# Tying a unit's attention scores behind the output of the unit two ahead

## The chip, the cores and the metric

One core of a Trainium2 chip runs the whole program. The metric is the device time of one execution in microseconds. The engines are TensorE (PE, with its weight loads as PEld), VectorE (DVE), ScalarE (ACT), GpSimd (POOL) and SyncE (SP), each with a queue of its own that it works off in order.

## The reference, cut to what matters

```python
# 1. attention: batch 4, 8 heads, 576 positions, head size 64
scores = q @ k.T / sqrt(64)
# heads 0-3: only the last 32 positions count ("local")
# heads 4-7: only positions of the same residue mod 32, not later ("strided")
attn = softmax(where(mask, scores, -1e9))
x = attn @ v                      # 2304 tokens x 512
# 2. a gated network: rms norm, 512 -> 2 x 1536 -> 512
xn = x / sqrt(mean(x*x) + 1e-6) * rms_g
x = (silu(xn @ w_gate) * (xn @ w_val)) @ w_out
# 3. a mixture of 8 experts, the best one for each token, 512 -> 1024 -> 512
out = p_e * (relu(x @ w1[e]) @ w2[e])
```

## The kernel before, in words

Attention is cut into 48 units, 12 for each batch: first six of the strided heads, then six of the local ones. A unit is a pair of heads and a group of 2, 3 or 4 tiles. In every tile the masked-out blocks are left out: a strided tile has 54 keys (L179 writes 64 x 54 scores), a local one 96 (64 x 96). The four steps of a unit are functions of their own:

- `scores`: two matmuls for each tile (one per head), from the tile `qk` into a PSUM bank (L179, `s<-qk` or `pt<-qk` in the profile); DVE adds the mask and takes the maximum (L189), ACT takes the exponential (L199). It also issues a later unit's load on SP's queue.
- `norm`: DVE divides by the sum (L220 to L222).
- `transpose`: a PE transpose for each tile (L228), and an ACT copy into the tile `ptS` (L230).
- `output`: two matmuls for each tile, `ptS` against `v` (L238, `mx<-ptS,v` or `o<-ptS,v`); ACT copies the result into the tile that the network reads (L247, L253).

The matmuls of attention are plain fp32, and each leaves two records in the trace: the 8 matmuls of a unit with 4 tiles are 16 records. The contraction of an output is over the keys, 54 or 96 rows; that of the scores over 64 rows.

The network works on nine chunks j of 256 tokens, each with 12 blocks f: `gate_val` is 24 matmuls of 256 columns (L472 to L474), `gelu_post` runs on ACT and DVE, `ff_out` is 6 matmuls of 512 columns (L497 to L499), two blocks later. These are called the main stream below. Units 0 to 11 are worked before it starts; units 12 to 47 are woven into it: three times in each block a `slot` is traced, which takes one or no piece from the list of `att_sequence`. Units 12 to 23 are the first such list (scores in the one bank `pt`, transposes and outputs in `mx`), 24 to 47 the second (scores in `s0` and `s1` in turn, transposes in `pt`, outputs in `mx`). In the list, two units ahead:

```python
for n in range(len(fs) + AHEAD):
    m = n - AHEAD + 1
    def piece(n=n, m=m):
        if 0 <= m < len(fs):
            fs[m][1]()           # norm of unit n-1
        if n < len(fs):
            fs[n][0]()           # scores of unit n
    seq.append(piece)
    if n >= AHEAD:
        seq += fs[n - AHEAD][2:] # transpose and output of unit n-2
```

An output can carry a number `after`: it isn't taken from the list before that chunk's inputs have been traced, since it overwrites a tile that they read. The order in which each engine gets its instructions isn't the order of tracing. A scheduler sets it before the run: by its own estimate of times it takes, for each engine, the instruction traced first among those that are ready. `tc.high_priority()` puts what is traced in it ahead of everything; `tc.issue_after(ins)` queues what is traced in it, on the engine of `ins`, behind `ins`, without waiting for its end. PE then works its queue strictly in that order, and an instruction that must wait for another engine holds all behind it.

Of the kernel before, what the change touches and what calls it, by code (L numbers as in the profile page):

```python
# [33 lines left out]
LQ, LK, SQ = 64, 64 + WIN, 3 * LEN  # L34
# [14 lines left out]
def moe_kernel(  # L49
# [17 lines left out]
    V, A, G, T, SP = nc.vector, nc.scalar, nc.gpsimd, nc.tensor, nc.sync  # L67
# [39 lines left out]
    units = []  # L107
# [9 lines left out]
    def fill(dst, n):  # L117

        for _ in range(n):
            T.matmul(dst, ones16, ones16, start=True, stop=True)  # L120
# [3 lines left out]
    def geometry(u):  # L124

        b, p, g = units[u]
        tiles = L_TILES if p < 2 else S_TILES
        return tiles[g], sum(tiles[:g]), *((LQ, LK) if p < 2 else (SQ, SQ))

    def load_part(c):  # L130
        u = n_load[c]
        if u >= len(units):
            return
        n_load[c] += 1
        b, p, g = units[u]
        n, t0, _, nk = geometry(u)
        if c == 0:
            cols = L_COLS if p < 2 else S_COLS
            w, o = cols[g], sum(cols[:g])
            if 3 <= u < 6:  # L140
                t = xn_p.tile([128, 2 * CH], F32, tag=("xh0", "xl0", "xh1")[u - 3], name="qk_early")
            else:
                t = qkv_p.tile([128, L_COLS[0]], F32, tag="qk", name="qk", bufs=3)
            SP.dma_start(out=t[:, :w], in_=(qk_l if p < 2 else qk_s)[b, p % 2, :, o:o + w])
        else:
            if 2 <= u < 8:
                if u % 2 == 0:
                    v_pair[0] = wts.tile([128, 2, 4, 128], F32, tag=f"w{NP - u // 2}", name="v_early")
                t = v_pair[0][:, u % 2]
            else:  # L150
                t = qkv_p.tile([128, 4, 128], F32, tag="v", name="v", bufs=2)
            SP.dma_start(
                out=t[:nk, :n],
                in_=(v_l if p < 2 else v_s)[b, p % 2].rearrange("k (t d) -> k t d", d=128)[:, t0:t0 + n],
            )
        qkv_t[u, c] = t

    def attention(u, banks):

        b, p, g = units[u]  # L160
        local = p < 2
        n, t0, nq, nk = geometry(u)
        k0 = n * nq if local else n * nq + LQ - SQ
        st = {}

        def scores():
            t = qkv_t.pop((u, 0))
            pr = pp.tile([128, 4, LK], F32, tag="pr", name="pr", bufs=3)
            mx = sm.tile([128, 4], F32, tag="mx", name="mx")
            sd = sm.tile([128, 4], F32, tag="sd", name="sd")  # L170
            sps = banks("s")
            if n_fill[0] < 12:
                n_fill[0] += 1
                fill(sps[:, 384:], 10)
            sps = sps[:, :4 * LK].rearrange("p (t k) -> p t k", k=LK)
            for i in range(n):
                for h in range(2):
                    hp = slice(64 * h, 64 * h + 64)
                    T.matmul(  # L179
                        sps[hp, i, :nk],  # L180
                        t[hp, i * nq:i * nq + LQ],
                        t[hp, k0 + i * nq:k0 + i * nq + nk],
                        start=True,
                        stop=True,
                    )
            for i in range(n):
                mask = m_str if not local else (m_loc0 if g == 0 and i == 0 else m_loc)
                pv = pr[:, i, :nk]
                V.tensor_tensor_reduce(  # L189
                    out=pv,  # L190
                    in0=sps[:, i, :nk],
                    in1=mask[:, :nk],
                    op0=ALU.add,
                    op1=ALU.min,
                    scale=-0.125,
                    scalar=3.0e38,
                    accum_out=mx[:, i:i + 1],
                )
                act = A.activation(  # L199
                    out=pv,  # L200
                    in_=pv,
                    func=AF.Exp,
                    bias=mx[:, i:i + 1],
                    scale=-1.0,
                    accum_out=None if u < 12 else sd[:, i:i + 1],
                )
                if not flow_on:
                    mark[0] = act
            st["p"] = pr, sd
            if not 3 <= u < 6:  # L210
                load_part(0)
            if u < 4:
                load_part(1)

        def norm():
            pr, sd = st["p"]
            pv, sl = pr[:, :n, :nk], sd[:, :n]
            if u < 12:
                V.tensor_reduce(out=sl, in_=pv, op=ALU.add, axis=AX.X)
            V.tensor_scalar(out=sl, in0=sl, scalar1=1e-9, scalar2=None, op0=ALU.add)  # L220
            V.reciprocal(out=sl, in_=sl)
            V.tensor_tensor(out=pv, in0=pv, in1=sl.unsqueeze(2).to_broadcast([128, n, nk]), op=ALU.mult)  # L222

        def transpose():
            pr, _ = st.pop("p")
            pt = banks("t").rearrange("p (t k) -> p t k", k=128)
            for i in range(n):
                T.transpose(pt[:nk, i], pr[:, i, :nk], ident)  # L228
            ptS = st["t"] = pp.tile([128, 4, 128], F32, tag="ptS", name="ptS", bufs=2)
            A.copy(ptS[:nk, :n], pt[:nk, :n])  # L230

        def output():
            t = qkv_t.pop((u, 1))
            ptS = st.pop("t")
            ot = banks("o")
            for i in range(n):
                for h in range(2):
                    T.matmul(  # L238
                        ot[64 * h:64 * h + 64, i * nq:(i + 1) * nq],
                        t[:nk, i, 64 * h:64 * h + 64],  # L240
                        ptS[:nk, i, 64 * h:64 * h + nq],
                        start=True,
                        stop=True,
                    )
            if local:
                x = x_t[b, p, g] = xt_p.tile([128, n * LQ], F32, tag=f"x{g}", name=f"x{g}", bufs=2)
                A.copy(x, ot[:, :n * LQ])  # L247
            else:
                if g == 0:
                    x_t[b, p] = xt_p.tile([128, S], F32, tag="xs", name="xs", bufs=4)  # L250
                x = x_t[b, p].rearrange("p (j c) -> p c j", c=CLS)
                c0, c1 = 3 * t0, min(3 * (t0 + n), CLS)
                A.copy(x[:, c0:c1], ot[:, :(c1 - c0) * LEN].rearrange("p (c j) -> p c j", j=LEN))  # L253
            if not 2 <= u < 8:
                load_part(1)
            n_out[0] = u + 1


        if local and b > 0:
            output.after = (S * (b - 1) + LQ * (t0 + n) - 1) // CH  # L260
        elif not local and b > 1:
            output.after = (S * (b - 1) - 1) // CH
        return scores, norm, transpose, output

    def att_sequence(us, banks):

        AHEAD = 2
        seq = []
        fs = [attention(u, banks) for u in us]
        for n in range(len(fs) + AHEAD):  # L270
            m = n - AHEAD + 1

            def piece(n=n, m=m):
                if 0 <= m < len(fs):
                    fs[m][1]()
                if n < len(fs):
                    fs[n][0]()

            seq.append(piece)
            if n >= AHEAD:  # L280
                seq += fs[n - AHEAD][2:]
        return seq
# [403 lines left out]
    stage = [0]  # L686
    turn = {"s": 0, "t": 0, "o": 0}

    def att_banks(kind):
# [7 lines left out]
        return bank((("mx", "o1")[n % 2], "mx", "mx")[stage[0]])  # L697

    aux = att_sequence(list(range(12)), att_banks)
    aux.reverse()  # L700
    fill(bank("mx")[:, :128], 40)
# [18 lines left out]

    hold.append(r_last[0])
    stage[0] = 1
    aux = att_sequence(list(range(12, 24)), att_banks)
    aux.reverse()
    rest = att_sequence(list(range(24, len(units))), att_banks)

    def pop_aux():
        if not aux and rest:
# [533 lines left out]
```

## Time and profile before

| what | value |
|---|---|
| three runs | 874.0, 875.13 and 1648.38 us; median 875.13 us |
| the profiled execution | 872.97 us, its span from first to last instruction 871.1 us |
| PE matmuls | 850.5 us busy, 98% of the span, 6872 records |
| PE weight loads | 764.1 us busy, 88% (beside the matmuls) |
| DVE, ACT, POOL | 509.1, 382.9 and 87.4 us busy: 58%, 44%, 10% |
| granted TensorE clock | 0.99 of full speed over the span |

Busy time of an engine is the time in which one of its instructions runs. A matmul's record is longer than the distance between two of them, since they overlap: what a matmul costs is read from start to start. The highest of the three runs isn't used.

### The profile page before, as it was taken

The numbers are of one execution on the slowest core, as the hardware profiler recorded it, in microseconds if no ns is written. First come the engines' busy times: TensorE is split into PE (matmuls) and PEld (weight loads), VectorE is DVE, ScalarE is ACT, GpSimd is POOL, SyncE is SP. The second block draws the span as 40 slices with busy tenths as digits, with TensorE's granted clock in tenths as the row PEclk, the third lists the DMA queues.
The fourth block names the chain that finished last, engine by engine and source line by source line (L and its number), as shares of the span: only waits on it lengthen the run. The fifth ranks groups of instructions, "written<-read, shape, count | busy, mean of one in ns | idle before, by whom it ended". The sixth has DMA issues, their size and how long they took to land.

```text
span 871.1 us, 18007 instructions
## 1 busy us (share of the span) xinstructions
PE 850.5 (98%) x6872; PEld 764.1 (88%) x6872; DVE 509.1 (58%) x1614; ACT 382.9 (44%) x935; POOL 87.4 (10%) x87
## 2 busy tenths in 40 slices
PE   8799999999999999999999999999999999999996
PEld 7588988988888988989999999998899999999995
DVE  4989974454653553644534535347786666666651
ACT  4766553344453254442332222325455545455540
POOL 0314500000000000000000000001031111111100
PEclk9889999999999999999999999999999999999998
DMA  8969111022121011100000000033196733765000
GB/s 251 351 224 329 68 32 41 11 59 60 36 61 53 1 47 44 61 14 26 1 10 26 1 21 5 2 125 118 62 365 216 217 129 113 230 214 183 25 25 21
DMA packets 33014, 84.45 MB, mean 97 GB/s; under 512 B 5122, under 2 KB 12850, under 8 KB 32920
## 3 DMA queue, kind: packets, MB, share of 16 engines
q1 hardware_dynamic: 23064, 54.50, 19.6%
q10 hardware_dynamic: 6336, 19.26, 6.0%
q0 software_dynamic: 3520, 9.45, 3.2%
q8 instruction: 58, 0.95, 0.4%
q14 instruction: 36, 0.29, 0.1%
HBM read 91.57 MB, written 10.49 MB: 117 GB/s over the span
## 4 chain that ended last, share of the span: by engine, by line
PE 81%; issue 10%; DMA 3%; DVE 2%; POOL 1%; ACT 1%; SPq 0%; ACTq 0%; POOLq 0%
PE gv L472 12%; PE gv L473 11%; PE gv L474 11%; PE o L499 5%; PE o L497 5%; PE o L498 5%; PE o L1023 3%; PE o L1025 3%; PE o L1024 3%; PE mx L238 2%; PE s L179 2%; PE s L999 2%; PE s L1000 2%; PE s L1001 2%; PE gv L999 2%
## 5 line engine op out<-in xcount | busy, mean ns | idle before, releaser
L472 PE MATMUL gv<-xh,wf 128*128 128x256 f32 x864 | 251.7, 292 | 0.8 <-DVE t L482 0.8
L473 PE MATMUL gv<-xl,wf 128*128 128x256 f32 x864 | 245.1, 284 | 0.0
L474 PE MATMUL gv<-xh,wf 128*128 128x256 f32 x864 | 244.5, 283 | 0.0
L472 PEld LDWEIGHTS gv<-xh,wf 128*128 128x128 f32 x864 | 163.3, 189 | 9.1 <-DVE t L482 1.7
L473 PEld LDWEIGHTS gv<-xl,wf 128*128 128x128 f32 x864 | 163.4, 189 | 3.3 <-issue 0.2
L474 PEld LDWEIGHTS gv<-xh,wf 128*128 128x128 f32 x864 | 163.6, 189 | 0.6 <-issue 0.2
L966 DVE TENSOR_TENSOR l<-stg,h 128x1024 fp32r<-128x1024 f32 x88 | 107.2, 1224 | 38.8 <-ACT h L965 38.6
L481 DVE SCALAR_TENSOR_TENSOR t<-t,gv 128x256 f32<-128x256 f32 x108 | 45.2, 418 | 121.5 <-ACT t L480 120.9
L965 ACT CAST h<-stg 128x1024 fp32r<-128x1024 f32 x88 | 91.6, 1048 | 35.8 <-PE o L1025 25.9
L480 ACT ACTIVATE t<-gv 128x256 f32<-128x256 f32 x108 | 41.3, 382 | 145.8 <-PE gv L474 135.8
L497 PE MATMUL o<-wf,hh 128*128 128x512 f32 x192 | 76.9, 400 | 0.0
L485 ACT CAST hh<-t 128x256 fp32r<-128x256 f32 x108 | 43.7, 405 | 73.8 <-PE o L499 31.9
L498 PE MATMUL o<-wf,hh 128*128 128x512 f32 x192 | 75.7, 394 | 0.0
L499 PE MATMUL o<-wf,hl 128*128 128x512 f32 x192 | 75.4, 398 | 0.0
L486 DVE TENSOR_TENSOR hl<-t,hh 128x256 fp32r<-128x256 f32 x108 | 48.6, 450 | 39.3 <-ACT hh L485 37.5
L1023 PE MATMUL o<-h,hT 128*128 128x512 f32 x176 | 70.6, 401 | 0.0
L1025 PE MATMUL o<-h,hT 128*128 128x512 f32 x176 | 68.8, 391 | 0.0
L1024 PE MATMUL o<-l,hT 128*128 128x512 f32 x176 | 68.5, 389 | 0.0
L199 ACT ACTIVATE pr<-pr,mx 128x54 f32<-128x54 f32 (+1 forms) x160 | 52.5, 348 | 14.3 <-DVE mx L189 13.7
L949 POOL DMA_INDIRECT xg<-rows_d,gi x22 | 24.2, 1102 | 302.4 <-DVE gi L947 142.4
L999 PE MATMUL s<-xh,h 128*128 128x256 f32 x176 | 49.7, 282 | 0.0
L1000 PE MATMUL s<-xl,h 128*128 128x256 f32 x176 | 49.5, 281 | 0.0
(212 smaller groups left out, 1556.9 us busy)
## 6 DMA issues: line engine op xcount, KB each, us to landing
stg<-in SPq DMA_DIRECT2D x96, 512.0 KB
raw<-in ACTq DMA_DIRECT2D x36, 511.8 KB
rows_d<-x SPq DMA_DIRECT2D x18, 256.5 KB
qk<-in SPq DMA_DIRECT2D x14, 221.0 KB
qk<-in SPq DMA_DIRECT2D x8, 272.0 KB
qk<-in SPq DMA_DIRECT2D x8, 208.0 KB
v<-in SPq DMA_DIRECT2D x14, 108.0 KB
qk<-in SPq DMA_DIRECT2D x7, 167.0 KB
```

Source lines behind the costliest of these rows:

```text
L472: T.matmul(dst, wh[:, ks], xh[k], start=(k == order[0]), stop=False)
L473: T.matmul(dst, wh[:, ks], xl[k], start=False, stop=False)
L474: T.matmul(dst, wl[:, ks], xh[k], start=False, stop=(k == order[3]))
L497: T.matmul(o, h[:, ms], wh, start=(f == 0), stop=False)
L498: T.matmul(o, h[:, ms], wl, start=False, stop=False)
L499: T.matmul(o, l[:, ms], wh, start=False, stop=(f == NF - 1))
L965: A.copy(h, lt["stg", i])
L966: V.tensor_tensor(out=l, in0=lt["stg", i], in1=h.bitcast(F32), op=ALU.subtract)
L999: T.matmul(dst, w[0][:, k, cs_], xh, start=(k == 0), stop=False)
L1023: T.matmul(ys[t][m], hh, w[0][:, c], start=(q == 0 and c == 0), stop=False)
L1024: T.matmul(ys[t][m], hh, w[1][:, c], start=False, stop=False)
L1025: T.matmul(ys[t][m], hl, w[0][:, c], start=False, stop=(q == 3 and c == 1))
```

## The change: what it does

For units 12 to 47 the list has another order. The scores of unit n and the output of unit n-2 are one piece: first the output's matmuls, then the scores'. Both are traced at the highest priority, and the scores' matmuls are queued on PE behind the last matmul of the output. The transpose of unit n-2 stands in the list ahead of that piece, the normalisation of unit n-1 behind it. The first two units of a list have no output ahead in it; unit 12's scores, and those of unit 24, are queued behind the last output of the list before. `after` holds back the whole piece.

```diff
+    pv_last = [None]
+
+    def close_to(last):
+
+        near = ExitStack()
+        if stage[0]:
+            near.enter_context(tc.high_priority())
+            if last[0] is not None:
+                near.enter_context(tc.issue_after(last[0].ins))
+        return near
...
-            for i in range(n):
-                for h in range(2):
-                    hp = slice(64 * h, 64 * h + 64)
-                    T.matmul(
...
+            with close_to(pv_last):
+                for i in range(n):
+                    for h in range(2):
+                        hp = slice(64 * h, 64 * h + 64)
+                        T.matmul(
...
+            pv_last[0] = None
...
-            for i in range(n):
-                for h in range(2):
-                    T.matmul(
...
+            with close_to([None]):
+                for i in range(n):
+                    for h in range(2):
+                        pv_last[0] = T.matmul(
...
-    def att_sequence(us, banks):
+    def att_sequence(us, banks, close=False):
...
+        if close:
+
+            for n in range(len(fs) + AHEAD):
+                m = n - AHEAD
+                if m >= 0:
+                    seq.append(fs[m][2])
+
+                def both_tiles(n=n, m=m):
+                    if m >= 0:
+                        fs[m][3]()
+                    if n < len(fs):
+                        fs[n][0]()
+
+                if m >= 0 and hasattr(fs[m][3], "after"):
+                    both_tiles.after = fs[m][3].after
+                seq.append(both_tiles)
+                if 0 <= m + 1 < len(fs):
+                    seq.append(fs[m + 1][1])
+            return seq
...
-    aux = att_sequence(list(range(12, 24)), att_banks)
+    aux = att_sequence(list(range(12, 24)), att_banks, True)
...
-    rest = att_sequence(list(range(24, len(units))), att_banks)
+    rest = att_sequence(list(range(24, len(units))), att_banks, True)
```

## Rows read from the trace of the kernel before

**Rows 1.** Windows view; stretch, length, busy time (instructions) of PE, PEld, DVE, ACT, POOL:

```profile
48.00:180.00 132.00, 130.66 (x1098) 117.23 (x1097) 96.50 (x279) 67.04 (x194) 26.86 (x26) 0.99 0.32 112
180.00:455.00 275.00, 275.00 (x2418) 243.94 (x2417) 137.02 (x626) 114.57 (x380) 1.85 (x2) 1.00 0.13 37
```

**Rows 2.** Waits of PE from 48 to 455 us; total, times, longest:

```profile
PE mx L238 <- ACT ptS L230: 1.0, 1, 1.0
PE mx L228 <- ACT xs L253: 0.3, 1, 0.3
```

**Rows 3.** PE's timeline, local outputs alone; start, length, line, operands, records:

```profile
258.45 0.28 PE L474 MATMUL gv<-xh,wf 128*128 128x256 f32 x1
258.67 0.69 PE L238 MATMUL mx<-ptS,v 96*64 96x64 f32 x16
...
259.51 0.28 PE L473 MATMUL gv<-xl,wf 128*128 128x256 f32 x1
...
451.00 0.28 PE L474 MATMUL gv<-xh,wf 128*128 128x256 f32 x1
451.21 0.45 PE L238 MATMUL mx<-ptS,v 96*64 96x64 f32 x8
...
451.82 0.28 PE L473 MATMUL gv<-xl,wf 128*128 128x256 f32 x1
```

**Rows 4.** PE's timeline, scores and a strided output side by side, their alternation left out:

```profile
318.57 0.40 PE L499 MATMUL o<-wf,hl 128*128 128x512 f32 x1
318.90 0.49 PE L179 MATMUL s<-qk 64*64 64x54 f32 x9
319.18 0.26 PE L238 MATMUL mx<-ptS,v 54*64 54x54 f32 x1
...
320.19 0.28 PE L473 MATMUL gv<-xl,wf 128*128 128x256 f32 x1
```

**Rows 5.** PE's timeline, scores and a local output side by side:

```profile
375.40 0.39 PE L499 MATMUL o<-wf,hl 128*128 128x512 f32 x1
375.72 0.38 PE L179 MATMUL s<-qk 64*64 64x96 f32 x2
376.02 0.69 PE L238 MATMUL mx<-ptS,v 96*64 96x64 f32 x16
376.64 0.71 PE L179 MATMUL s<-qk 64*64 64x96 f32 x10
...
377.50 0.28 PE L473 MATMUL gv<-xl,wf 128*128 128x256 f32 x1
```

**Rows 6.** PE's timeline, the first attention piece inside the main stream:

```profile
55.64 0.44 PE L179 MATMUL pt<-qk 64*64 64x54 f32 x8
```

**Rows 7.** Timeline, transposes and the ACT copy behind them: units 17 and 31:

```profile
112.12 0.49 PE L228 MATMUL mx<-cs,pr 128*54 128x128 f32 x3
...
115.97 0.46 ACT L230 COPY ptS<-mx 54x384 f32<-54x384 f32 x1
...
254.98 0.60 PE L228 MATMUL pt<-cs,pr 128*96 128x128 f32 x4
...
255.75 0.58 ACT L230 COPY ptS<-pt 96x512 f32<-96x512 f32 x1
```

**Rows 8.** PE's timeline ahead of the main stream's first matmul:

```profile
42.36 1.10 PE L179 MATMUL pt<-qk 64*64 64x54 f32 x16 [0.51 <-ACT ptS L230]
43.39 0.69 PE L362 MATMUL gv<-cs,nr 128*128 128x128 f32 x2
44.23 1.10 PE L179 MATMUL pt<-qk 64*64 64x54 f32 x16 [0.15 <-PE gv L362]
...
45.74 0.64 PE L238 MATMUL o<-ptS,v 96*64 96x64 f32 x8
47.19 0.89 PE L179 MATMUL pt<-qk 64*64 64x54 f32 x12 [0.80 <-PE o L238]
48.01 0.80 PE L472 MATMUL gv<-xh,wf 128*128 128x256 f32 x2
```

More of the change, by code (lines that the diff above doesn't have):

```diff
@@ L175, in scores @@
             sps = sps[:, :4 * LK].rearrange("p (t k) -> p t k", k=LK)
-            for i in range(n):
-                for h in range(2):
-                    hp = slice(64 * h, 64 * h + 64)
-                    T.matmul(
[L180 to L185, printed above, removed]
+            with close_to(pv_last):
[3 more added lines that the diff above has]
+                        T.matmul(
+                            sps[hp, i, :nk],
+                            t[hp, i * nq:i * nq + LQ],
+                            t[hp, k0 + i * nq:k0 + i * nq + nk],
+                            start=True,
+                            stop=True,
+                        )
+            pv_last[0] = None
             for i in range(n):
@@ L235, in output @@
             ot = banks("o")
-            for i in range(n):
-                for h in range(2):
-                    T.matmul(
[L239 to L244, printed above, removed]
+            with close_to([None]):
+                for i in range(n):
+                    for h in range(2):
+                        pv_last[0] = T.matmul(
+                            ot[64 * h:64 * h + 64, i * nq:(i + 1) * nq],
+                            t[:nk, i, 64 * h:64 * h + 64],
+                            ptS[:nk, i, 64 * h:64 * h + nq],
+                            start=True,
+                            stop=True,
+                        )
             if local:
```

## The prediction

> **What bounds the kernel now.** I read the windows view first. TensorE (PE) is busy 130.66 of 132 us in the stretch from 48 to 180 us and 275.00 of 275 us from 180 to 455 us, while DVE and ACT have room [rows 1]. These two stretches hold every attention piece of units 12 to 47 but the scores of units 12, 13 and 14, so the second view to read is who PE waited for in them: 1.3 us in all, 1.0 of it once, for the copy of a transposed tile [rows 2]. Nothing but PE's own queue sets the time there. A main matmul less or more on PE moves the end by its own length, and so does whatever an attention piece costs PE beyond its own columns. The third view is therefore PE's timeline: how much later does the main stream come back after a piece?
>
> Main matmuls of 256 columns start 0.118 us apart, those of 512 columns 0.233 us. Take the 16 records of one output of K=96 (each fp32 matmul leaves two records): from the last main start, 258.45, to the second main start behind, 259.51, pass 1.06 us; two ordinary steps would take 0.24, so the piece cost 0.82. The same form with 8 records costs 451.82 - 451.00 - 0.24 = 0.58 [rows 3]. The difference is 0.03 us per record, which leaves 0.34 us that do not depend on the number of records: 0.17 us for going from main work into the piece and 0.17 us for coming back. Call each a change.
>
> Two places show what happens when scores and outputs stand side by side already. Strided: 16 scores and 16 outputs of K=54, mixed with one another, cost 320.19 - 318.57 - 0.35 = 1.27 us [rows 4]; 32 x 0.03 is 0.96, so two changes of 0.155 and none inside, however often the lines alternate. Local: 2 scores, 16 outputs of K=96, 10 scores cost 377.50 - 375.40 - 0.35 = 1.75 us [rows 5]; with 0.045 for a record of 96 columns (0.03 x 96/64) the columns are 12 x 0.045 + 16 x 0.03 = 1.02, and 0.73 is left, which is four changes of 0.18. So going between scores (64 rows by 64) and a local output (96 rows by 64) is a change as dear as one to main work; between scores and a strided output (54 rows by 64) it is free.
>
> The Trainium skill, "TensorEngine Tiling (Array Packing)", section "Key Properties", says that changing the tiling mode, not merely the tile, drains TensorE. Read that way it speaks against the change for the local pairs, whose two halves differ in mode; the rows agree, at 0.18 us. Were the two halves one mode, the 14 local pairs below would each save 0.17 more, 2.4 us in all.
>
> **The change part by part.** It removes and adds no matmul; it moves them. *Ties.* Scores of unit n (n from 14 to 23 and from 26 to 47) are queued on PE behind the last output matmul of unit n-2, and both are picked ahead of all main work once ready. Today each stands where the scheduler found room, and pieces are cut in two: of unit 15's 16 score records 8 stand at 55.64 [rows 6] and 8 behind later main work.
>
> Counting on PE's timeline, the attention pieces from 55.64 [rows 6] to 451.21 [rows 3] make 66 stretches between main matmuls (a stretch beside transposes counts once; the transposes themselves show no change price and stay). Eight of these have two changes inside, like [rows 5]. That is 66 x 2 + 8 x 2 = 148 changes. After: 32 pairs; 4 outputs alone (units 22, 23, 46, 47); the scores of 24 and 25 alone, since they start the second sequence; and the scores of unit 13, see below. That is 39 stretches, 78 changes, and 14 more inside the local pairs (outputs 18 to 21, 30 to 35, 42 to 45): 92. Fewer by 56, at 0.17 us: 9.5 us saved.
>
> *Scores that lose their cover.* Units 12, 13 and 14 now run at 42.36, 44.23 and 47.19, before the main stream's first matmul at 48.01 [rows 8], where PE has idle time. Unit 12's will wait behind unit 11's output (45.74) and still fit before the main stream. Unit 13's need the same PSUM bank as unit 12's, read out by DVE in between, and land inside the stream: 16 x 0.03 = 0.48 us of columns (its two changes are counted above). Unit 14's ride behind unit 12's output: 12 x 0.03 = 0.36 us. Together 0.84 us lost. Net 9.5 - 0.8 = 8.7 us.
>
> *The start itself.* Unit 12's scores at 42.36 stand ahead of the matmul that spreads the first norm (43.39), on which all of the main stream's inputs hang [rows 8]. With them gone that matmul could start up to 1.0 us earlier. Against that, unit 12's scores may now push the first main matmul back by their own length, 1.1 us. I take nothing, with both ends, -1.0 and +1.1, in the range.
>
> *The new wait.* An output at the highest priority is queued on PE directly behind the moment at which the scheduler expects the ACT copy of the transposed tile. If the copy is later on the chip, all of PE waits: main matmuls are behind it in an in-order queue. Today there is room: unit 31's transposes end at 255.58, its copy at 256.33 [rows 7], and its output starts at 258.67 [rows 3], 2.3 us behind. Such an undisturbed copy is over 0.75 us after the transposes, in some six main matmuls. A disturbed one, unit 17's, only starts 3.36 us after them (112.61 and 115.97), behind other ACT work [rows 7]. So a wait is bounded by 0 and by about 3.2 us (3.36 + 0.46 less the 0.6 that six matmuls and a start take) for each pair. The trace has one output close behind its copy, unit 12's, and it waited 1.0 us [rows 2]; all else that PE consumes in these 407 us was in time within 0.3 us [rows 2]. I lean to the many: 0.05 us for each of 32 pairs, 1.6 us.
>
> *Queues passed.* The loads that a score or output issues on SP's queue stay in program order with the piece that holds them; a score now comes two slots later and its next load with it, and three buffers cover that. The normalisation of a unit is now one slot ahead of its transposes, not four; its three small DVE instructions have a slot of 1.4 us there (a third of 24 x 0.118 + 6 x 0.233). ACT gets the output's copy and DVE the scores' maxima at once; both had idle time there [rows 1]. I cost these at nothing; if DVE's cover fails between 48 and 130 us, the first to be late is a transpose, and PE waits for it as it does for the copy.
>
> *Sum.* The profiled execution took 872.97 us (span 871.1). 872.97 - 8.7 + 1.6 = 865.9. The two runs that agree, 874.0 and 875.13, are 1.0 and 2.2 above the profiled one, so I add 1.3 and say 867 for a median.
>
> **The rivals.** *A: the wait takes the place of the gap, and the kernel is slower.* Place: the ten pairs of the first sequence (outputs 12 to 21), where DVE and ACT are busiest and copies come late. If the schedule foresees nothing of ACT's queue, each waits like unit 12's, 1.0 us: +10 against -8.7, 1.3 slower, 876. It decides from 0.87 us for each of the ten pairs, or 0.27 us for each of all 32. For it: unit 12's wait and unit 17's late copy. Against: one such wait in 407 us. Half of it, 0.15 us for every pair, gives 865.9 + 3.2 + 1.3, about 870.5.
>
> *B: the tie doesn't bind.* The edge only orders scores behind outputs; if they are not ready then (bank not yet read out by DVE, load not landed), main matmuls get in between and the pair is two stretches. Then only cut pieces are healed: 7 extra stretches and the 16 inner changes, 14 + 16 = 30 changes, 5.1 us, less 0.8 and some waits: about 871. For it: the first sequence has one scores bank. Against: a unit takes six slots there, over 8 us, and the bank's last reader is DVE at the start of that time.
>
> *C: more than forecast.* The start gains its 1.0 us, and the 1.3 us of waits [rows 2] go because less DVE work stands ahead of them; no pair waits: 872.97 - 8.7 - 2.3 + 1.3, about 863.
>
> **How the numbers follow.** Forecast 0.55 (its own range 864 to 870); A in half 0.15 (870.5); A in full, slower than before, 0.08 (876); B 0.09 (871); C 0.13 (863). The range from 862 to 875 leaves out A in full and a little on either end. Two per cent, about what a measurement of this kernel can tell from no change, is 17.5 us: no case reaches that. I keep 0.04 for faster by more (the changes would have to cost twice what the rows show), 0.03 for slower by more (waits of over 0.8 us for every pair), 0.93 within.
>
> **What would show it.** On PE's timeline scores directly behind outputs in 32 places; 16 + 16 strided records at about 1.3 us, local ones at 1.4 to 1.7 us with three changes; about 39 stretches. PE's waits for ACT's copy between 48 and 455 us at 1 to 4 us in all; 10 or more is rival A. Main matmuls between an output and its scores are rival B. The first main matmul near 48. Behind 455 us everything as before, some 7 us earlier. I am wrong if the pairs are in place and the end has not moved: then PE was not the only bound.

## The result and the profile after

The changed kernel takes 867.11 us, median of four runs (865.1 to 868.9). The kernel before has three usable runs, 874.0, 875.13 and 877.93 us, with a mean of 875.7 (a fourth was disturbed and isn't used). The ratio is 0.9902, 95% interval 0.9875 to 0.9928: 8.6 us less, between 6.3 and 10.9. Run once more later it gave 0.988 (0.9851 to 0.9909), 10.5 us less. The prediction said 867.

The head of the profile page (busy us, share of the span, instructions) shows TensorE as full as before, in a span that is 5.7 us shorter:

```profile
span 865.4 us, 18024 instructions
PE 843.9 (98%) x6872; PEld 763.8 (88%) x6872; DVE 508.9 (59%) x1614; ACT 381.5 (44%) x935; POOL 85.7 (10%) x87
```

PE has the same 6872 records and 6.6 us less to be busy with; no work was taken out, so the work itself got cheaper on PE. The windows view of the same two stretches (columns as in [rows 1]) shows where: in the same 407 us PE now gets through 3599 matmul records instead of 3516.

```profile
48.00:180.00 132.00, 129.50 (x1118) 117.68 (x1115) 97.66 (x299) 69.57 (x209) 25.09 (x26) 0.98 0.34 116
180.00:455.00 275.00, 274.69 (x2481) 247.94 (x2479) 139.55 (x631) 114.36 (x384) 1.85 (x2) 1.00 0.13 37
```

PE's timeline shows how. A strided pair, to be held against [rows 4], and then a local one, against [rows 5]:

```profile
344.27 0.28 PE L507 MATMUL gv<-xh,wf 128*128 128x256 f32 x1
344.48 0.61 PE L252 MATMUL mx<-ptS,v 54*64 54x54 f32 x13
344.88 0.26 PE L191 MATMUL s<-qk 64*64 64x54 f32 x1
...
344.98 0.52 PE L191 MATMUL s<-qk 64*64 64x54 f32 x11
345.43 0.39 PE L505 MATMUL gv<-xh,wf 128*128 128x256 f32 x1
345.65 0.28 PE L506 MATMUL gv<-xl,wf 128*128 128x256 f32 x1
...
127.83 0.28 PE L507 MATMUL gv<-xh,wf 128*128 128x256 f32 x1
128.04 0.69 PE L252 MATMUL mx<-ptS,v 96*64 96x64 f32 x16
128.66 0.71 PE L191 MATMUL pt<-qk 64*64 64x96 f32 x12
129.30 0.39 PE L505 MATMUL gv<-xh,wf 128*128 128x256 f32 x1
129.53 0.28 PE L506 MATMUL gv<-xl,wf 128*128 128x256 f32 x1
```

By the prediction's method (last main start to second main start behind, less two steps of 0.12) the strided pair costs 1.14 us: 28 records at 0.03 are 0.84, and 0.30 is left for two changes. The local pair costs 1.46: 1.02 of columns and 0.44, three changes of 0.15. Counted in PE's order from the first main matmul on, there are 38 stretches of attention with 15 inner changes, 91 changes in all, against the 148 of before; the prediction expected 39, 14 and 92. The three differences: the scores of units 24 and 25 stand together (one stretch less), output 13 and its scores are parted by main work (one more), and two pairs, with the outputs of units 34 and 35, stand in one stretch (one less, and one inner change more).

PE's waits from 48 to 455 us (total, times, longest) answer to [rows 2]:

```profile
PE gv L505 <- DVE t L515: 1.4, 2, 1.2
PE gv L505 <- ACT xh L410: 0.9, 2, 0.7
PE mx L252 <- ACT ptS L243: 0.2, 1, 0.2
```

2.5 us in place of 1.3. 0.7 of them stand in front of the very first main matmul; of the copy `ptS`, which the prediction feared, 0.2 us is left.

The last view is PE's timeline ahead of the main stream, against [rows 8]:

```profile
41.90 0.88 PE L375 MATMUL gv<-cs,sq 128*128 128x1 f32 x4
...
45.34 0.69 PE L395 MATMUL gv<-cs,nr 128*128 128x128 f32 x2 [0.71 <-DVE nr L389]
...
48.84 0.80 PE L505 MATMUL gv<-xh,wf 128*128 128x256 f32 x2 [0.73 <-ACT xh L410]
```

The row at 41.90 is the sum of squares of the first norm, from which the main stream's inputs follow; call it the root. In the kernel before it is this row:

```profile
39.12 0.87 PE L342 MATMUL gv<-cs,sq 128*128 128x1 f32 x4
```

So the main stream begins 6.94 us behind the root instead of 8.89. The root itself came 2.78 us later, and with it the stream, at 48.84 instead of 48.01. That is no effect of the change: PE's and DVE's instructions up to the root are the same, in the same order, in both kernels.

From the first main matmul to the last of `ff_out` the stream takes 557.6 us before and 550.2 us after; behind it lie about 257 us in both. Within the stream there is one more difference, in the granted clock of its first microseconds (windows, first before, then after):

```profile
48.00:51.00 3.00, 3.00 (x16) 2.99 (x15) 2.61 (x13) 2.98 (x16) 0.00 (x0) 0.51 0.34 94
51.00:54.00 3.00, 3.00 (x27) 3.00 (x27) 1.74 (x7) 0.44 (x2) 0.00 (x0) 1.00 0.29 31
```

```profile
48.00:51.00 3.00, 2.27 (x12) 1.93 (x9) 2.40 (x12) 2.83 (x13) 0.00 (x0) 0.50 0.45 134
51.00:54.00 3.00, 3.00 (x21) 2.87 (x21) 1.42 (x5) 0.83 (x6) 0.00 (x0) 0.56 0.00 0
```

The stream ran at the lower level (1.2 of 2.4 GHz) for 2.9 us before and for 4.8 us after, with PE idle for 0.73 us just ahead of it in the second. At half the clock half of these times is lost: 1.45 and 2.4 us. Without them the stream is 556.2 and 547.8 us long, a gain of 8.4 us.

### The profile page after: what moved, and what is told of

It is laid out like the page before. It is cut to its first block, busy times and chain, and to the rows that moved or that the text cites. A ratio compares the mean times of both kernels' runs of the same rounds, so it can differ in the third digit from the quotient of the medians.

```text
span 865.4 us, 18024 instructions
## 1 busy us (share of the span) xinstructions
PE 843.9 (98%) x6872; PEld 763.8 (88%) x6872; DVE 508.9 (59%) x1614; ACT 381.5 (44%) x935; POOL 85.7 (10%) x87
## 4 chain that ended last, share of the span: by engine, by line
PE 76%; issue 11%; DVE 7%; DMA 3%; ACT 1%; POOL 1%; ACTq 0%; POOLq 0%; DVEq 0%; SPq 0%
PE gv L505 11%; PE gv L506 11%; PE gv L507 10%; PE o L530 5%; PE o L531 5%; PE o L532 5%; PE o L1056 3%; PE o L1058 3%; PE o L1057 3%; PE mx L252 2%; PE s L1032 2%; DVE wf L458 2%; PE s L1033 2%; PE s L1034 2%; PE gv L1032 2%
```

## The experiments

The theory: PE is the bound, and an attention piece costs 0.17 us for every change between main, 64-row and 96-row work; the time falls with the number of changes, and the order of tracing and the priority matter only as far as they alter that number. The rivals: (A) the gain comes from the other order in the list, or from the priority, because units run earlier; (B) it comes from the start of the main stream alone. Each kernel was run 4 to 12 times; ratios are to the kernel before on the same chip, and microseconds are that ratio times 876. The stream's length is from the profiled run.

| kernel | changes | ratio [95%] | us against before | stream, us |
|---|---|---|---|---|
| before | 148 | 1 | 0 | 557.6 |
| changed, first / again | 91 | 0.9902 [0.9875, 0.9928] / 0.988 [0.9851, 0.9909] | -8.6 / -10.5 | 550.2 / 549.9 |
| order of the list only | 143 | 0.9992 [0.9976, 1.0008] | -0.7 | 556.0 |
| tie without priority | 95 | 0.9896 [0.9871, 0.9921] | -9.1 | 550.9 |
| priority without tie | 153 | 1.0039 [1.002, 1.0059] | +3.4 | 560.4 |
| units 24 to 47 only | 105 | 0.9922 [0.9897, 0.9946] | -6.8 | 550.0 |
| local outputs with 64 rows | 91, 15 of them free | 0.9867 [0.9836, 0.9899] | -11.6 | 547.6 |
| a matmul inside each pair | 139 | 0.995 [0.9931, 0.9969] | -4.4 | 555.9 |
| scores of 12 and 13 untied | 89 | 0.9928 [0.9902, 0.9953] | -6.3 | 553.1 |
| wide local outputs | about 70 | 0.9921 [0.9891, 0.9951] | -6.9 | 553.2 |
| two units at a time, two banks | 67 | 0.9877 [0.9846, 0.9909] | -10.8 | 549.8 |
| two units at a time, one bank | 63 | 0.988 [0.9852, 0.9907] | -10.5 | 551.1 |
| the same, norms in another bank | 63 | 0.9983 [0.9965, 1.0002] | -1.5 | 558.8 |

**The list without tie and priority.**

```diff
-        if stage[0]:
+        if False:
             near.enter_context(tc.high_priority())
```

> The list in its new order, but neither the tie nor the priority. The scheduler's queue for PE then has 143 changes between attention and other work from the main stream's first matmul on, against 148 before and 91 after. Theory (each change costs PE 0.17 us, and their number makes the difference): 5 x 0.17 = 0.9 us faster than before, so within 2 us of it. Rival (the new list order gains, by giving copies and normalisations more room, and the ties do little): most of the 9 us, 6 to 9 us faster than before.

Measured: ratio 0.9992 [0.9976, 1.0008]. Five changes fewer would be 0.85 us; 0.7 was found, which cannot be told from nothing. The new order of the list is not the cause.

**The tie without the priority.**

```diff
-            near.enter_context(tc.high_priority())
             if last[0] is not None:
                 near.enter_context(tc.issue_after(last[0].ins))
```

> The list in its new order and the scores queued behind the output, without the priority. PE's queue has 95 changes against 148 before and 91 after. Theory (number of changes): 53 x 0.17 = 9.0 us less 0.8 us for the scores of units 13 and 14 that lose their cover: 8 us faster than before, 0.7 us slower than the changed kernel. Rival (the priority is what gains, because an output no longer stands behind main work): 0 to 3 us faster than before.

Measured: 0.9896 [0.9871, 0.9921], the same as the whole change within the intervals. The priority adds nothing to the tie that shows.

**The priority without the tie.**

```diff
             near.enter_context(tc.high_priority())
-            if last[0] is not None:
-                near.enter_context(tc.issue_after(last[0].ins))
```

> The list in its new order and the priority for both, without the tie. PE's queue has 153 changes, five more than before: scores are ready sooner than the output and go ahead alone, or in two parts around it. Theory (number of changes): 0.9 us slower than before, within 2 us of it. Rival (the priority is what gains): 5 to 9 us faster than before.

Measured: 1.0039 [1.002, 1.0059], 3.4 us slower than before. PE's timeline shows what two pieces of equal priority do to each other:

```profile
257.29 0.39 PE L528 MATMUL o<-wf,hh 128*128 128x512 f32 x1
257.61 0.32 PE L189 MATMUL s<-qk 64*64 64x54 f32 x2
257.86 0.33 PE L250 MATMUL mx<-ptS,v 96*64 96x64 f32 x2
...
261.39 0.33 PE L250 MATMUL mx<-ptS,v 96*64 96x64 f32 x2
261.65 0.50 PE L529 MATMUL o<-wf,hh 128*128 128x512 f32 x1
```

Scores of a strided unit and a local output take turns, matmul by matmul, eight times. From 257.29 to 261.65, less one step of 0.23, are 4.13 us; the 32 records at 0.03 are 0.96, so 17 changes cost 3.17, 0.19 each. The windows view of the same kernel shows a second price (columns as in [rows 1]):

```profile
257.00:262.00 5.00, 5.00 (x39) 3.71 (x39) 1.02 (x3) 0.63 (x2) 0.00 (x0) 1.00 0.00 0
262.00:266.00 4.00, 4.00 (x19) 3.56 (x18) 1.41 (x8) 1.73 (x7) 0.00 (x0) 0.57 0.33 93
```

Right behind this stretch the granted clock falls from 1.00 to 0.57 for 4 us: 3.4 us at the lower level, 1.7 us lost. PE was not idle before the fall; it was changing. 0.85 for five changes more and 1.7 for the clock are 2.6 us of the 3.4; the rest lies within the interval. The theory as stated expected less than was found, since it had no term for the clock.

**Only the second list changed.**

```diff
-        if stage[0]:
+        if stage[0] == 2:
...
-    aux = att_sequence(list(range(12, 24)), att_banks, True)
+    aux = att_sequence(list(range(12, 24)), att_banks)
```

> The change for units 24 to 47 alone; units 12 to 23 keep the old list, so the scores of units 12, 13 and 14 run ahead of the main stream again. PE's queue has 105 changes. Theory (number of changes): 43 x 0.17 = 7.3 us faster than before, and nothing lost at the start: 7.3 us, some 1.5 us slower than the changed kernel. If the later start of the main stream in the changed kernel's profile (48.84 against 48.01 us) and its later rise of the clock come from the change, this one has them back, 2 us more: 9.3 us faster than before.

Measured: 0.9922 [0.9897, 0.9946], 6.8 us for 43 changes fewer (7.3 by their price). The scores of units 12, 13 and 14 run ahead of the main stream again, in the order of before, and the stream alone is 7.6 us shorter in the profiles (550.0 against 557.6), so the start cannot be the cause of these. (The stream begins 8.36 us behind the root here and in the kernel with the priority alone, not 8.89. The order is that of before; the root's four records took 0.60 to 0.61 us there and 0.87 before.)

**Local outputs in the scores' mode.**

```diff
-                            t[:nk, i, 64 * h:64 * h + 64],
-                            ptS[:nk, i, 64 * h:64 * h + nq],
+                            t[:min(nk, 64), i, 64 * h:64 * h + 64],
+                            ptS[:min(nk, 64), i, 64 * h:64 * h + nq],
```

> The changed kernel, with the local outputs contracted over 64 of their 96 keys (the last 32 keys of a local tile are left out of the product with v), so that they use 64 rows by 64 as the scores do; columns, records and PE's queue stay as they are. Theory (going between 96 rows and 64 rows is a change of 0.17 to 0.18 us, between 54 or 64 rows and 64 rows it is free): the 15 changes inside local pairs go, 2.6 us faster than the changed kernel; a local pair of 16 and 12 records costs 1.28 us in place of 1.46. Rival (what a pair costs hangs on its columns and on entering and leaving alone): no difference.

Measured: 0.9867 [0.9836, 0.9899]. On PE's timeline a local pair now looks like this:

```profile
130.32 0.28 PE L507 MATMUL gv<-xh,wf 128*128 128x256 f32 x1
130.53 0.62 PE L252 MATMUL mx<-ptS,v 64*64 64x64 f32 x13
...
131.85 0.28 PE L506 MATMUL gv<-xl,wf 128*128 128x256 f32 x1
```

131.85 - 130.32 - 0.24 = 1.29 us instead of 1.46, with the same number of columns: the inner change is gone, at 0.16 to 0.17. Fifteen of these are 2.5 us; the stream is 2.6 us shorter. The ratio's interval overlaps with that of the changed kernel, so it is the rows and the stream that show it, not the time of the whole. The Trainium skill, "TensorEngine Tiling (Array Packing)", section "Key Properties", says that a change of mode drains the engine where a change of tile doesn't; these rows agree, and put 0.17 us to it.

**A matmul of 128 columns put into each pair.** It stands between output and scores and undoes the joining without moving either.

```diff
+    bank_of = [None]
...
+            bank_of[0] = sps
...
             with close_to(pv_last):
+                if stage[0] and pv_last[0] is not None and u not in (12, 24):
+                    fill(bank_of[0][:, 384:], 1)
                 for i in range(n):
```

> The changed kernel with one bf16 matmul of 128 rows, 128 by 128 into unused columns of the scores' bank, between the output and the scores of each tied pair: the tie stays, the pair is parted by work of the main stream's mode. PE's queue has 139 changes in place of 91. Theory (number of changes): 48 x 0.17 = 8.2 us, and 31 to 33 fillers of some 0.06 us, 1.9 us: 10 us slower than the changed kernel, 1 us slower than before. Rival (the gain comes from the place of the pieces in the stream, not from their touching): 2 us slower than the changed kernel.

Measured: 0.995 [0.9931, 0.9969], 4 to 6 us slower than the changed kernel, half of what was expected. PE's timeline, a strided pair of the form shown above:

```profile
347.19 0.28 PE L511 MATMUL gv<-xh,wf 128*128 128x256 f32 x1
347.40 0.67 PE L256 MATMUL mx<-ptS,v 54*64 54x54 f32 x16
348.00 0.23 PE L120 MATMUL s<-ones 128*128 128x128 bf16 x1
348.16 0.56 PE L195 MATMUL s<-qk 64*64 64x54 f32 x12
348.65 0.38 PE L509 MATMUL gv<-xh,wf 128*128 128x256 f32 x1
348.87 0.28 PE L510 MATMUL gv<-xl,wf 128*128 128x256 f32 x1
```

It costs 1.44 us instead of 1.14. Half a main matmul of 256 columns, 0.06, is the filler's own length by estimate; 0.24 is left for two changes. So the direction holds, but this change is cheaper, 0.12 us, than one to main work. The 14 local pairs lose about 0.16 each (one change more: 1.62 against 1.46), and 17 joined strided pairs x 0.30 + 14 x 0.16 = 7.3 us is what the rows give; the times show 4 to 6, with intervals of about 2, and the profiled stream 5.7 to 5.9. PE's waits inside the stream take 0.5 to 0.7 us off (1.1 us here, 1.6 to 1.8 in the changed kernel).

**The scores of units 12 and 13 left untied.**

```diff
-            with close_to(pv_last):
+            with close_to(pv_last) if u not in (12, 13) else ExitStack():
```

> The changed kernel, with the scores of units 12 and 13 neither tied nor at the highest priority, so that they run ahead of the main stream again. PE's queue behind the main stream's first matmul has two changes and 16 records fewer. Theory: 0.8 us faster than the changed kernel. If unit 12's scores ahead of the spread of the first norm cost the start as much as they save, no difference.

Measured: 0.9928 [0.9902, 0.9953], 2 to 4 us slower than the changed kernel, with intervals that touch; 0.8 us faster was expected. Its main stream begins 8.07 us behind the root, 1.1 us more than in the changed kernel, because these scores stand ahead of the spreading of the norm again (0.83 us of it). PE's waits inside the stream are 3.2 us, 1.3 to 1.6 more than in the changed kernel (1.0 once, for ACT's copy `xs`). Together, and less 0.8 us for two changes and 16 records fewer, these are 1.6 to 1.9 us. The profiled run, 873.91 us, is the slowest of six (median 870.67), and in it the clock costs more: its root came late, at 44.79, the stream began at 52.86, and the windows view from 54 to 60 us shows the lower level where the changed kernel, in the second row, has the full one:

```profile
54.00:60.00 6.00, 5.91 (x29) 5.91 (x30) 2.34 (x8) 2.07 (x9) 0.00 (x0) 0.54 0.04 11
```

```profile
54.00:60.00 6.00, 6.00 (x62) 5.92 (x61) 5.09 (x30) 2.57 (x12) 0.08 (x1) 1.00 0.74 213
```

All its six runs were granted less than most of the changed kernel's (0.976 to 0.984 of full speed over the span, against 0.981 to 0.989 in ten). Why, and how much of the 2 to 4 us that is, stays open.

**Local outputs as one wide matmul for each tile**, to take them from the mode of 96 rows by 64 to the main one; only the two diagonal blocks are copied out.

```diff
+            wide = ot.rearrange("p (t c) -> p t c", c=128)
...
-                for h in range(2):
+                    if local:
+                        pv_last[0] = T.matmul(wide[:, i], t[:nk, i], ptS[:nk, i], start=True, stop=True)
+                    for h in () if local else range(2):
...
-                A.copy(x, ot[:, :n * LQ])
+                for h in range(2):
+                    hp = slice(64 * h, 64 * h + 64)
+                    A.copy(x[hp].rearrange("p (t c) -> p t c", c=LQ), wide[hp, :n, 64 * h:64 * h + 64])
```

> The changed kernel, with a local tile's output as one matmul of 96 rows by 128 columns for both heads (the two diagonal blocks are copied out, the other two are computed and dropped), in place of two of 96 rows by 64. Theory (a piece that uses over 64 rows and 128 columns is in the main stream's own mode and pays no change): a local pair keeps the two changes of its scores, the lone outputs of units 22, 23, 46 and 47 keep none; 21 changes fewer than the changed kernel, 3.6 us, and 108 records of 128 columns (some 0.055 us) for 216 of 64 (0.03), 0.6 us less: 4.2 us faster than the changed kernel. Rival (every fp32 attention piece pays for entering and leaving, whatever rows and columns it uses): 0.6 us faster.

Measured: 0.9921 [0.9891, 0.9951], 3.6 us slower than the changed kernel beside it, where the theory had 4.2 faster; the intervals overlap. PE's timeline, one such output with two tiles:

```profile
181.29 0.28 PE L512 MATMUL gv<-xh,wf 128*128 128x256 f32 x1
181.41 0.61 PE L253 MATMUL mx<-ptS,v 96*128 96x128 f32 x4
181.77 0.36 PE L510 MATMUL gv<-xh,wf 128*128 128x256 f32 x1
181.97 0.28 PE L511 MATMUL gv<-xl,wf 128*128 128x256 f32 x1
```

It begins one ordinary step, 0.12 us, behind the main matmul ahead of it, and costs 181.97 - 181.29 - 0.24 = 0.44 us, which is its four records and nothing else, so the change is gone. But the records lie 0.11 us apart and not the 0.055 that I had taken: 108 wide records cost 11.9 us where 216 narrow ones cost 6.5. 21 changes fewer, 3.6 us, don't pay for 5.4; 0.7 to 1.0 us more of waits inside the stream (2.6) and a slower clock at its start make up most of the rest. The claim about the mode holds; the kernel built on it was sized wrongly.

**Two units at a time.** For units 24 to 47 two outputs and two scores are tied in a row, so that every second pair of changes goes; the outputs use the banks `mx` and `pt` in turn. Its core:

```diff
...
+            def four_tiles(n=n, m=m):
...
+                    fs[m + 1][3]()
+                    chain[0] = True
+                    fs[m][3]()
...
+                    fs[n][0]()
+                    chain[0] = False
+                    fs[n + 1][0]()
...
```

> The changed kernel, with units 24 to 47 taken two at a time: outputs m+1 and m, then the scores of m+2 and m+3, all four tied and at the highest priority; the second output uses the bank pt. PE's queue has 67 changes in place of 91. Theory (number of changes): 24 x 0.17 = 4.1 us faster than the changed kernel, 13 us faster than before, if PE waits nowhere. Rival (longer blocks make copies and normalisations late, so that PE waits): less than 1 us faster than the changed kernel, or slower.

Measured: 0.9877 [0.9846, 0.9909]. 24 changes fewer than in the changed kernel, and no time gained that shows: the rival's case. Two of the doubles were split again by the bank `pt`, so both outputs were put into the halves of `mx`, their copies behind both:

```diff
...
-                    fs[m + 1][3]()
+                    o2 = banks("o")
+                    fs[m + 1][4](o2[:, 256:])
                     chain[0] = True
-                    fs[m][3]()
+                    fs[m][4](o2[:, :256])
+                    fs[m][5]()
+                    fs[m + 1][5]()
...
```

> Units 24 to 47 two at a time, as in the earlier double, but both outputs in the two halves of the bank mx, so that neither waits for the bank pt, and both copied out behind the four tied pieces. PE's queue has 63 changes, against 91 in the changed kernel and 67 in the earlier double. Theory (number of changes, with PE's waits as in the changed kernel): 28 x 0.17 = 4.8 us faster than the changed kernel. Rival (blocks of two units make PE wait for copies and for the bank, as in the earlier double, where 2.8 us of waits came up in two places): 1 to 2 us faster than the changed kernel.

Measured: 0.988 [0.9852, 0.9907], against 0.988 for the changed kernel run again, so even the rival's 1 to 2 us don't show. The waits of PE from 45 to 455 us say where most of the 4.8 us of 28 changes went:

```profile
PE mx L257 <- ACT r L438: 1.5, 2, 1.0
...
PE mx L257 <- ACT ptS L244: 1.2, 2, 1.0
PE mx L436 <- DVE nr L430: 1.0, 1, 1.0
```

With the four rows not shown all waits come to 6.8 us; 5.4 of them are inside the stream, against 1.6 in the changed kernel run again. That is 3.8 of the 4.8 us. The bank `mx`, which the norms of the chunks use as well, is what the matmuls of these three rows write. So the norms of the later chunks were moved to `pt`:

```diff
-            ss = bank("mx") if j else bank("gv", 2)
+            ss = bank("pt" if j > 2 else "mx") if j else bank("gv", 2)
...
-            bc = (bank("mx") if j else bank("gv", 2))[:, :CH]
+            bc = (bank("pt" if j > 2 else "mx") if j else bank("gv", 2))[:, :CH]
```

> The double with both outputs in one bank, and the norms of chunks 3 to 8 (two small matmuls and two transposes) moved from the bank mx to the bank pt, so that a block of two units no longer finds mx held by the copy of a norm. PE's queue has 63 changes. Theory (what the doubles failed to gain went into PE's waits for that bank): the waits for the norm's DVE and ACT steps from 180 to 455 us, 1.5 and 1.0 us in the double before, go, and it is 2.5 us faster than that one, 3 to 4 us faster than the changed kernel. Rival (the waits only change their name): within 1 us of the double before.

Measured: 0.9983 [0.9965, 1.0002]: nearly the whole gain is gone. It is 9 us slower than the double before, so the theory is wrong and even the rival, who had it within 1 us, was too hopeful. The norm now shares `pt` with the transposes of attention. First the longest waits of PE from 45 to 455 us, then the windows around the longest of them:

```profile
PE gv L546 <- ACT xh L451: 4.9, 3, 3.1
PE pt L436 <- DVE nr L430: 1.7, 1, 1.7
```

```profile
380.00:384.00 4.00, 0.97 (x6) 0.72 (x7) 3.61 (x17) 3.53 (x16) 0.00 (x0) 1.00 0.14 44
384.00:390.00 6.00, 6.00 (x39) 6.00 (x40) 1.28 (x3) 0.79 (x2) 0.00 (x0) 0.72 0.01 3
```

PE stood idle for 3 of 4 us, and then the clock was at its lower level for 3.4 of the next 6. This happened twice (the other time at 313 us, 3.4 us as well): 10.3 us of waits in place of 6.8, and 3.4 us lost to the clock, make 6.9 of the 7.7 us by which this stream is longer than that of the kernel above.

**The changed kernel once more**, beside the wide outputs:

> The changed kernel once more, beside the one with wide local outputs: 0.9902 of before within the interval, 8.6 us faster, and the same waits of PE as in its first profile if they belong to its schedule; the main stream's start at another time if that belongs to the run.

Measured: 0.988 [0.9851, 0.9909]. PE waits in the same three rows as in the first profile (1.2, 0.9 and 0.2 us), so they belong to the schedule. The root came at 40.80 instead of 41.90 in the same kernel, so its time belongs to the run.

## Why the prediction was right

The time was 867 as forecast, and by the mechanism that it named. That it was met to the microsecond is luck in part: two terms of the sum were too cautious by 3 us together, and the base to which they were added was some 2 us too low.

*The changes.* 57 fewer were counted after, 56 forecast. The 148 of before came out right by luck: PE's order has 70 stretches, four of them with two changes inside like [rows 5], where the prediction read 66 and eight. Removing them by halves (second list only), putting them back (the list alone, the priority alone, the matmul inside each pair) and taking the inner ones away (64-row outputs) all moved the time or the stream in step with their number, the matmul inside each pair at a lower price than the others. This is shown, not only argued, down to the changed kernel's 91; below that number the doubles' saving went into waits. Rival A of the experiments fell with the list alone and with the priority alone; rival B with the second list alone.

*The lost cover.* The trace has 464 score records in the stream instead of 436: the 28 records of units 13 and 14, which are 0.84 us at 0.03 each, as forecast.

*The tie.* It binds in 31 of 32 pairs, so the prediction's rival B (it doesn't bind) is out. The one pair with main work inside looks like the case that rival B describes:

```profile
66.66 0.67 PE L252 MATMUL mx<-ptS,v 54*64 54x54 f32 x16 [0.20 <-ACT ptS L243]
...
70.58 0.67 PE L191 MATMUL pt<-qk 64*64 64x54 f32 x16
```

These are output 13 and the scores of unit 15, which need the one bank `pt`; DVE read it until 68.72. That priority makes the pieces early, which the prediction took for granted, is wrong: without it the order is nearly the same (95 changes against 91).

*The new wait: mis-sized.* The prediction had it at 1.6 us: "An output at the highest priority is queued on PE directly behind the moment at which the scheduler expects the ACT copy". Mostly it isn't. PE's and ACT's timeline for unit 36:

```profile
313.03 0.60 PE L241 MATMUL pt<-cs,pr 128*54 128x128 f32 x4
313.66 0.58 ACT L243 COPY ptS<-pt 54x512 f32<-54x512 f32 x1 [0.70 <-PE pt L241]
...
316.64 0.61 PE L252 MATMUL mx<-ptS,v 54*64 54x54 f32 x14
```

The copy ends at 314.24 and its output starts 2.4 us behind, much as in [rows 3, 7]. Only units 12, 13 and 16 follow within 0.25 us, and one of these waited, 0.2 us. The waits inside the stream rose by 0.5 us, to 1.8, and for another reason (gelu's `t`, once 1.2). The prediction's rival A had no place to act.

*The start: mis-sized.* The prediction took nothing, with ends of -1.0 and +1.1. From the root to the first main matmul the kernel before needs 8.89 us and the list-only kernel 8.90; the changed kernel needs 6.94 both times, and so do the tie without priority, the 64-row outputs, the inserted matmul and all the doubles, within 0.01. That is 1.95 us gained in each of these profiles. 0.83 of it is what the prediction named, the spreading of the norm freed of unit 12's scores (3.44 us behind the root instead of 4.27). The other 1.12, from the spreading to the stream, it did not see. The kernel with units 12 and 13 untied splits it, since there only unit 14's scores have left the place ahead of the stream: from the spreading to the first main matmul it needs 3.79 us, against 4.62 before and 3.51 in the changed kernel. So 0.83 us is due to unit 14's scores, which stood directly ahead of the first main matmul (47.19 and 48.01 in [rows 8]) although the prediction had them under cover; 0.28 us is the work of units 12 and 13 (that it is their exponentials on ACT and maxima on DVE among the first chunk's casts is not shown). The root itself came between 39.1 and 44.8 us in the profiled runs, behind the same PE instructions in the same order but for the two kernels with other local outputs, and in the two profiles compared above this hid the gain.

*The sum by measured terms*, in us (waits and clock from the profiled run: PE's waits inside the stream beyond the 1.3 of before, and half the time at the lower clock inside it beyond the 1.5 of before):

| kernel | changes x 0.17 | cover | start | waits | clock | sum | measured |
|---|---|---|---|---|---|---|---|
| changed | -9.7 | +0.8 | -1.95 | +0.5 | +0.9 | -9.4 | -8.6 and -10.5 |
| tie only | -9.0 | +0.8 | -1.95 | +1.1 | +0.6 | -8.4 | -9.1 |
| list only | -0.85 | 0 | 0 | 0 | -0.2 | -1.1 | -0.7 |
| second list only | -7.3 | 0 | 0 | +0.2 | 0 | -7.1 | -6.8 |
| priority only | +0.85 | 0 | 0 | -0.5 | +1.8 | +2.1 | +3.4 |
| double, one bank | -14.5 | +0.8 | -1.95 | +4.1 | +0.7 | -10.8 | -10.5 |

The forecast of -7.1 was thus some 3 us too cautious, 1.6 - 0.5 in the wait and 1.95 in the start; the lower clock at the stream's start, for which it had no term, took back 0.9 in the first profile and 0.3 when the kernel was run again. The prediction's rival C, 863, had the start right in kind. That 867 was met nonetheless is owed to the base: the profiled execution of before, 872.97, was faster than each of its other runs at the time (874.0 to 877.93), with the earliest root of all profiles, and its medians beside the experiments were 875.7 to 876.8. So adding 1.3 us for the median was too little by about 2.

*Behind 455 us* nothing changed but the moment: 257 us from the end of the stream to the last matmul in both.

What stays open: the part of the 2 to 4 us, beyond the start and the waits, by which the kernel with units 12 and 13 untied falls behind, and why the root's time differs by up to 5.7 us from run to run. No kernel tried does the whole computation and beats the changed one by more than the intervals.

## What to carry to other kernels

When an in-order engine is full, price what it does between its instructions: take the time from the last main start before a small piece to the main start behind it, subtract the columns, and see what is left for each change of shape. Join pieces of one shape by an order that binds, not by priority: two pieces of equal priority were dealt out in turns and cost more than both apart. Stop when the saving comes back as waits: here the step from 91 to 63 changes gave 4.8 us to PE, waits took back 3.8, and no gain showed in the time.

## What the runs showed of the hardware

- A change between main work and a piece of 54, 64 or 96 rows by 64 costs TensorE 0.15 to 0.17 us, between 64-row scores and a 96-row output 0.15 to 0.19 us, and about 0.12 us where the matmul between them is a single bf16 one of 128 columns. 54 and 64 rows by 64 share a mode, 96 rows by 64 do not share theirs, and 96 rows by 128 showed no change against main work.
- The granted clock fell from 1.00 to the lower level in a running stream at two kinds of places: behind 4 us of work with 17 changes, in which PE counts as fully busy (0.57 over the next 4 us), and behind idle time of PE: 3 us within 4 (0.72 over the next 6 us), and, with units 12 and 13 untied, two waits of 0.8 and 1.0 us close to each other (0.57 from 73 to 77 us). Single waits of 1.0 and 1.2 us, before and after the change, were followed by no fall.
- A plain fp32 matmul with 128 columns of weights and 128 columns of data leaves records 0.11 us apart (4 in 0.44 us), where those with 64 columns of weights and 64 columns of data are 0.03 us apart.
